# Loading q and k by blocks of 32 tokens with four heads in one DMA, and issuing v half a slot behind its buffer's use

## The chip, the cores and the metric

The kernel runs on one core of a Trainium2 chip. The metric is the device time of one execution in microseconds (us), as the median of several runs. Besides, one execution was taken with the hardware profiler; its trace is what the rows below come from. Times inside the trace count from the start of its span.

## The reference

Attention within chunks of 64 tokens, then two feed-forward layers one after the other. All inputs are float32 but the four weight arrays and alpha, which are float64 on the host.

```python
# q, k, v: (8 batches, 8 heads, 576 tokens, 64)
scores = 1/sqrt(64) * q_c @ k_c^T            # in chunks of 64 tokens
attn = exp(scores - max); attn = attn / (sum(attn) + 1e-9)
out = attn @ v_c
x = out as (8 * 576 = 4608 tokens, 512)      # heads side by side
h = x @ w_in;   x = (h * sigmoid(1.702 h)) @ w_out          # 512 -> 2048 -> 512
h = x @ w_in2;  y = (max(h, 0) + alpha * min(h, 0)) @ w_out2
```

## The kernel before

**Groups, blocks, slots.** Attention works on 36 groups `g` of 128 tokens (`NG`, line 73). A batch has 576 tokens, which is four and a half groups, so the groups 4, 13, 22 and 31 straddle two batches: 64 tokens of one, 64 of the next. The first feed-forward layer works on 9 blocks of 512 tokens (four groups each), and each block has 16 slots `n`, one for each 128 columns of the hidden layer. In a slot TensorE makes 12 matmuls of `emit_h` (line 454) and 12 of `emit_y` (line 477). The second layer (lines 601 to 868) follows when the first is done, and nothing in it is touched here.

**Attention between the slots.** The attention of the groups from 4 on is threaded into the slots by hand: the table `between` (lines 930 to 941) says at which half slot a step of group `g` is emitted, counted from `8 * (g - 4)`. An even half slot lies in the middle of `emit_h` (`middle`, line 951), an odd one behind `emit_y` (line 970). `att_T` (-4) transposes q and k on VectorE (line 325), `att_S` (-1) makes the scores on TensorE (line 341), `att_E` (-1) the exponentials, `att_AT` (2) transposes them, `att_PV` (5) multiplies with v on TensorE (line 410), after which ScalarE copies the result into the layer's input (line 418).

**The loads.** All DMAs are issued by SyncE (SP in the rows), strictly in the order in which the program emits them. `load_qk` (line 285) loads q and k of a group in eight parts, q in parts 0 to 3, k in parts 4 to 7, one part at each half slot from -1 to 6, two groups ahead. In the tile (128 partitions by 512) the partition is 32 columns `y` of a head of even or odd number, so that VectorE's transposes of 32 by 32 give what TensorE needs; line 298 therefore issues one DMA for each head, each `y`, and each batch that the group touches: 4 DMAs of 16 KB in a part, and 8 of 8 KB in a part of a straddling group. The tiles of q and of k have two buffers each, and the first DMA of a tile waits until `att_T` has read the group two before. `load_v` (line 282, issue at line 276) loads v of the next group into the single buffer of v, so it waits for the matmuls of `att_PV`; it is emitted at half slot 7. Groups 4 and 5 are loaded by another list (`LOADS`, line 20), so `load_qk` serves groups 6 to 35, of which 13, 22 and 31 straddle.

**What else is in SP's queue.** The first layer's weights (lines 132 and 137) during the first block; from slot 19 to slot 123, once in 3.25 slots, a step that prepares the second layer's weights: two loads of raw weights (line 202), which ScalarE reads two slots later (line 152), and two stores (line 208) of what ScalarE and GpSimd have made of them; and at each block's end four stores of the layer's result (line 491).

**Order within one half slot.** The list at a half slot holds its steps in the order in which the loop over `g` adds them. With v at half slot 7, the queue of SP has part 7 of k (group g + 2), then v (group g + 1), then part 0 of q (group g + 3).

Of the kernel before, what the change touches and what calls it, by code (L numbers as in the profile page):

```python
# [17 lines left out]
SQ = 32  # L18
# [30 lines left out]
def tile_chunk_attention_two_ffn(  # L49
# [14 lines left out]
    nc = tc.nc  # L64
    B, H, S, D = q.shape
    NT, DM = out.shape
    DFF = w_in1.shape[1]
    P = 128
# [3 lines left out]
    GPB = NB // P  # L72
# [172 lines left out]
    def spans(t0, n):  # L245
        done = 0
        while done < n:
            b, s = divmod(t0 + done, S)
            step = min(n - done, S - s)
            yield done, step, b, s  # L250
            done += step
# [33 lines left out]
    def load_qk(part, g):  # L285

        nm, src = (("q", q), ("k", k))[part // 4]
        if part % 4 == 0:  # L290
            t = qkv_p.tile([P, 512], F32, tag=nm, name=nm, bufs=2)
            qkv[g, nm] = t.rearrange("p (h b e) -> p h b e", h=HP, e=SQ)
        t = qkv[g, nm]
        for h in range(part % 4 * 2, part % 4 * 2 + 2):
            for y in range(D // SQ):
                r = (h % 2) * D + y * SQ
                for off, n, b, s in spans(g * P, P):
                    nc.sync.dma_start(  # L298
                        out=t[r:r + SQ, h // 2, off // SQ:(off + n) // SQ],
                        in_=src[b, h, s:s + n, y * SQ:(y + 1) * SQ].rearrange(  # L300
                            "(b t) e -> t b e", t=SQ
                        ),
                    )

    qkT = {}

# [563 lines left out]
    with tc.manual_schedule():  # L870
# [50 lines left out]
        for i, step in enumerate(steps):  # L921
            n = PREP_FROM + int(i * PREP_EVERY)
# [7 lines left out]
        between = {}  # L930
        for g in range(GPB, NG):
            for at, fn in zip((-4, -1, -1, 2, 5), (att_T, att_S, att_E, att_AT, att_PV)):
                if g > GPB or at > 0:
                    between.setdefault(8 * (g - GPB) + at, []).append((fn, g))
            if g + 1 < NG:
                between.setdefault(8 * (g - GPB) + 7, []).append((load_v, g + 1))
            if g + 2 < NG:
                for part in range(8):
                    between.setdefault(max(0, 8 * (g - GPB) - 1 + part), []).append(
                        (partial(load_qk, part), g + 2)  # L940
                    )
# [83 lines left out]
```

## Time and profile before

| | us |
|---|---|
| median of 3 runs | 1686.51 |
| the three runs | 1685.52 to 1688.97 |
| the profiled execution | 1682.19 |
| its span in the trace | 1680.4 |
| TensorE busy in it | 1610.9 |
| VectorE busy in it | 1243.7 |

The profiled execution is 4.3 us below the median of the runs, and 1.8 us of it lie outside the span. The first layer ends near 930 us of the span, the second takes the rest. In the rows, PE is TensorE, PEld its weight loads, DVE VectorE, ACT ScalarE, POOL GpSimd, SPq the queue of SyncE, by which the DMAs are issued. The duration of a DMA in SPq is the time that SyncE spent on issuing it, not the transfer.

### The profile page before, as it was taken

How to read it: one execution, taken by the hardware profiler on the slowest of the kernel's cores; microseconds unless marked ns; L12 is line 12 of the kernel's file. 1: busy time of each engine (PE TensorE's matmuls, PEld its weight loads, DVE VectorE, ACT ScalarE, POOL GpSimd, SP SyncE). 2: the span in 40 equal slices, each digit the busy share in tenths (PEclk: the TensorE clock that was granted, in tenths of full speed). 3: DMA queues.
4: the chain of work that ended last, by engine and by line, in shares of the span. 5: the costliest groups of instructions: out<-in, count | busy, mean ns of one | idle time of the engine just before them, and what ended most of it. 6: DMA issues, size and time to landing. Idle time of an engine off the chain costs nothing.

```text
span 1680.4 us, 25742 instructions
## 1 busy us (share of the span) xinstructions
PE 1610.9 (96%) x9259; PEld 1342.0 (80%) x9259; DVE 1243.7 (74%) x1858; ACT 782.9 (47%) x1098; POOL 491.4 (29%) x382
## 2 busy tenths in 40 slices
PE   7889998999999999989999999999999999999997
PEld 5667886888877788778888778878887888899897
DVE  7898676677766877767744367987889789788776
ACT  5555344444434444435433364545555555445543
POOL 3665121322222222222202025322523332241220
PEclk8999998999999999999999999999999999999999
DMA  9741333445334444444330376669667866987974
GB/s 235 203 133 18 93 96 101 124 113 133 99 101 114 134 107 114 106 105 129 101 131 14 120 233 192 196 173 303 192 188 180 286 193 201 249 309 231 264 235 134
DMA packets 385582, 268.10 MB, mean 160 GB/s; under 512 B 265648, under 2 KB 323504, under 8 KB 385456
## 3 DMA queue, kind: packets, MB, share of 16 engines
q1 hardware_dynamic: 385456, 266.47, 55.4%
q8 instruction: 73, 1.20, 0.3%
q14 instruction: 53, 0.43, 0.1%
HBM read 218.11 MB, written 48.23 MB: 159 GB/s over the span
## 4 chain that ended last, share of the span: by engine, by line
PE 61%; DVE 16%; SPq 4%; ACT 4%; DMA 3%; issue 3%; POOL 0%; DVEq 0%; ACTq 0%; POOLq 0%
PE psY L477 16%; PE psH L454 15%; PE psHa L653 8%; PE psYa L770 8%; PE psYb L770 6%; PE psHb L653 6%; SPq L298 3%; DVE g L672 3%; DVE o L717 2%; DVE yacc L788 2%; DVE at L393 2%; PE psS L341 2%; DVE g L698 1%; DVE xop L566 1%; DVE g L463 1%
## 5 line engine op out<-in xcount | busy, mean ns | idle before, releaser
L454 PE MATMUL psH<-xs,wi 128*128 128x512 f32 x1728 | 439.3, 405 | 10.2 <-DVE g L463 5.9
L477 PE MATMUL psY<-gs,wo 128*128 128x512 f32 x1728 | 416.4, 391 | 0.1
L454 PEld LDWEIGHTS psH<-xs,wi 128*128 128x128 f32 x1728 | 330.2, 194 | 86.4 <-DVE g L463 9.3
L477 PEld LDWEIGHTS psY<-gs,wo 128*128 128x128 f32 x1728 | 325.4, 189 | 68.7 <-POOL gs L123 0.5
L120 ACT CAST gs<-g 128x512 fp32r<-128x512 f32 x144 | 89.3, 620 | 331.5 <-DVE g L463 331.5
L770 PE MATMUL psYa<-o,w 128*128 128x512 f32 (+1 forms) x960 | 216.2, 371 | 9.9 <-DVE o L717 3.6
L653 PE MATMUL psHa<-xop,wi2t 128*128 128x512 f32 (+1 forms) x960 | 211.8, 369 | 2.6 <-DVE g L698 1.9
L770 PEld LDWEIGHTS psYa<-o,w 128*128 128x128 f32 x960 | 173.7, 188 | 40.7 <-DVE o L717 10.6
L653 PEld LDWEIGHTS psHa<-xop,wi2t 128*128 128x128 f32 x960 | 175.1, 188 | 27.6 <-DVE g L698 2.7
L672 DVE SCALAR_TENSOR_TENSOR g<-neg,minus_alpha,g 128x512 f32<-128x512 f32 (+1 forms) x160 | 179.3, 1161 | 9.9 <-ACT g L669 9.7
L653 PE MATMUL psHb<-xop,wi2t 128*128 128x512 f32 (+1 forms) x720 | 158.8, 369 | 3.2 <-DMA wi2t<-wi 2.3
L770 PE MATMUL psYb<-o,w 128*128 128x512 f32 (+1 forms) x720 | 159.0, 368 | 0.1
L123 DVE TENSOR_TENSOR gs<-g,gs 128x512 fp32r<-128x512 f32 x129 | 91.9, 712 | 88.6 <-ACT gs L120 87.9
L463 DVE TENSOR_TENSOR g<-psH,g 128x512 f32<-128x512 f32 x144 | 98.1, 681 | 79.1 <-ACT g L461 78.2
L653 PEld LDWEIGHTS psHb<-xop,wi2t 128*128 128x128 f32 x720 | 131.3, 188 | 21.5 <-DMA wi2t<-wi 2.9
L722 POOL TENSOR_TENSOR tsum<-g,tsum 128x1024 f32<-128x1024 f32 (+1 forms) x39 | 93.0, 2384 | 187.8 <-DVE o L717 187.8
L722 POOL TENSOR_TENSOR tsum<-g,g 128x1024 f32<-128x1024 f32 (+1 forms) x19 | 42.6, 2243 | 356.0 <-DVE g L672 220.2
L770 PEld LDWEIGHTS psYb<-o,w 128*128 128x128 f32 x720 | 131.3, 188 | 18.2 <-DVE o L717 1.5
L393 DVE STREAM_TRANSPOSE at<-e 32x128 f32<-32x128 f32 x448 | 135.5, 302 | 6.7
L461 ACT ACTIVATE g<-psH 128x512 f32<-128x512 f32 x144 | 86.2, 599 | 74.3 <-PE psH L454 73.6
L668 ACT ACTIVATE neg<-g 128x1024 f32<-128x1024 f32 (+1 forms) x60 | 58.6, 976 | 122.2 <-DVE g L698 122.2
L367 POOL TENSOR_TENSOR e<-e,d 128x512 f32<-128x512 f32 x32 | 33.5, 1046 | 253.9 <-DVE d L366 235.9
(117 smaller groups left out, 1888.3 us busy)
## 6 DMA issues: line engine op xcount, KB each, us to landing
wi2t<-wi SPq DMA_DIRECT2D x280, 256.0 KB, 3.6
w<-wo SPq DMA_DIRECT2D x140, 512.0 KB, 3.8
x<-ysb SPq DMA_DIRECT2D x36, 256.0 KB, 2.6
raw<-in_moe_w_in_dram SPq DMA_DIRECT2D x16, 512.0 KB, 5.4
raw<-in_moe_w_out_dram SPq DMA_DIRECT2D x16, 512.0 KB, 4.3
raw<-in_moe_w_in_dram SPq DMA_DIRECT2D x32, 256.0 KB, 4.0
wi<-stb SPq DMA_DIRECT2D x16, 512.0 KB, 3.0
raw<-in_moe_w_out_dram SPq DMA_DIRECT2D x32, 256.0 KB, 3.6
```

The source lines that it names most:

```text
L120: nc.scalar.copy(hi, src)
L123: eng_lo.tensor_tensor(out=lo, in0=src, in1=hi.bitcast(F32), op=ALU.subtract)
L393: nc.vector.transpose(t[o * SQ:(o + 1) * SQ, :, i * SQ:(i + 1) * SQ], blocks[i * SQ:(i + 1) * SQ, :, o // 2, o % 2, :],)
L454: nc.tensor.matmul(ps, w[:, a, c], xs[:, b, c], start=(i == 0), stop=(i == 3 * KT - 1))
L461: nc.scalar.activation(out=g, in_=ps, func=AF.Sigmoid, scale=1.702)
L463: nc.vector.tensor_tensor(out=g, in0=ps, in1=g, op=ALU.mult)
L477: nc.tensor.matmul(y_t[j][t], w[:, a, t * P:(t + 1) * P], gs[:, b], start=(f == 0 and a + b == 0), stop=(f == NF - 1 and b == 1),)
L653: nc.tensor.matmul(ps, w[:, c, a], x[b][:, c], start=(k == 0 and i in (1, 2, 5)), stop=(k == 5 and i in (2, 3, 4)), skip_group_check=True,)
L668: nc.scalar.activation(out=neg, in_=src, func=AF.Relu, scale=-1.0)
L672: nc.vector.scalar_tensor_tensor(out=g, in0=neg, scalar=minus_alpha[:, f:f + 1], in1=g, op0=ALU.mult, op1=ALU.add)
L722: eng.tensor_tensor(out=wide(homes[out], n), in0=wide(homes[x], n), in1=wide(homes[y], n), op=ALU.subtract,)
L770: nc.tensor.matmul(ps[:, d, :n], w[:, jj, d, a], x[b][:, jj], start=(k == 0 and i in (1, 5, 2)), stop=(k == 5 and i in (3, 2, 4)), skip_gr ...
```

## The change

`load_qk` is rewritten: a part is now a block of 32 tokens instead of a pair of heads. It makes one DMA for each parity of the head number and each half `y` of the head's columns, and a DMA takes the four heads of that parity at once: 4 DMAs of 16 KB in every part of every group, straddling or not, since 32 divides 576 and no block of 32 tokens crosses a batch. The pieces of 128 bytes are as before; in the tile they now lie 512 bytes apart, in the input one head pair apart. Then `load_v` is emitted at half slot 6 instead of 7: in SP's queue v (group g + 1) goes ahead of part 7 of k (group g + 2).

```diff
-        for h in range(part % 4 * 2, part % 4 * 2 + 2):
+        off = part % 4 * SQ
+        b, s = divmod(g * P + off, S)
+        for par in range(2):
             for y in range(D // SQ):
-                r = (h % 2) * D + y * SQ
-                for off, n, b, s in spans(g * P, P):
-                    nc.sync.dma_start(
-                        out=t[r:r + SQ, h // 2, off // SQ:(off + n) // SQ],
-                        in_=src[b, h, s:s + n, y * SQ:(y + 1) * SQ].rearrange(
-                            "(b t) e -> t b e", t=SQ
-                        ),
-                    )
+                r = par * D + y * SQ
+                nc.sync.dma_start(
+                    out=t[r:r + SQ, :, part % 4],
+                    in_=src[b, par::2, s:s + SQ, y * SQ:(y + 1) * SQ].rearrange("h t e -> t h e"),
+                )
...
             if g + 1 < NG:
-                between.setdefault(8 * (g - GPB) + 7, []).append((load_v, g + 1))
+                between.setdefault(8 * (g - GPB) + 6, []).append((load_v, g + 1))
```

## Rows read from the trace of the kernel before

**Rows 1.** The page: busy us (share), instructions.
```profile
PE 1610.9 (96%) x9259; PEld 1342.0 (80%) x9259; DVE 1243.7 (74%) x1858; ACT 782.9 (47%) x1098; POOL 491.4 (29%) x382
```

**Rows 2.** Timeline, PE: att_PV of groups 11, 15, 19, 23, 27, 31, 35.
```profile
246.91 0.69 PE L410 MATMUL psX<-at,v 64*64 64x64 f32 x32
...
353.78 0.69 PE L410 MATMUL psX<-at,v 64*64 64x64 f32 x32
...
450.29 0.69 PE L410 MATMUL psX<-at,v 64*64 64x64 f32 x32
...
555.07 0.69 PE L410 MATMUL psX<-at,v 64*64 64x64 f32 x32
...
651.54 0.69 PE L410 MATMUL psX<-at,v 64*64 64x64 f32 x32
...
756.07 0.69 PE L410 MATMUL psX<-at,v 64*64 64x64 f32 x32
...
852.74 0.69 PE L410 MATMUL psX<-at,v 64*64 64x64 f32 x32
```

**Rows 3.** Waits of PE, 168 to 900 us: total, times, longest.
```profile
PE psS L341 <- ACT x L418: 9.4, 4, 4.4
PE psX L410 <- DMA v<-in_v_dram: 5.8, 3, 2.3
```

**Rows 4.** Busy us by stretch, PE to POOL, then PEclk, DMA share, GB/s.
```profile
235.00:269.00 34.00, 34.00 (x203) 27.16 (x202) 23.22 (x49) 14.27 (x25) 8.41 (x13) 1.00 0.28 67
269.00:291.00 22.00, 15.72 (x106) 12.30 (x105) 12.79 (x30) 5.67 (x10) 1.23 (x1) 0.77 0.53 148
315.00:340.00 25.00, 25.00 (x166) 20.32 (x165) 16.57 (x36) 11.72 (x19) 6.44 (x8) 1.00 0.47 120
```

**Rows 5.** Timeline of SP, straddling group 13: start, us, engine, line.
```profile
257.43 11.82 SPq L298 DMA_DIRECT2D k<-in_k_dram  x24
269.35 0.39 SPq L276 DMA_DIRECT2D v<-in_v_dram  x1
...
280.45 1.54 SPq L202 DMA_DIRECT2D raw<-in_moe_w_in_dram  x2
```

**Rows 6.** Timeline of SP in a group that doesn't straddle.
```profile
409.91 2.02 SPq L298 DMA_DIRECT2D k<-in_k_dram  x4
412.03 0.38 SPq L276 DMA_DIRECT2D v<-in_v_dram  x1
```

**Rows 7.** Timeline of PE there: att_PV of groups 17 and 18.
```profile
402.44 0.69 PE L410 MATMUL psX<-at,v 64*64 64x64 f32 x32
...
426.37 0.69 PE L410 MATMUL psX<-at,v 64*64 64x64 f32 x32
```

**Rows 8.** Timeline of ACT, straddling group 22; in brackets the idle time.
```profile
506.14 0.67 ACT L152 ACTIVATE u<-raw 128x512 f32<-128x512 f32 x1 [7.69 <-DMA q<-in_q_dram]
```

**Rows 9.** Timeline of DVE: the transpose of group 19's q.
```profile
426.18 0.70 DVE L325 STREAM_TRANSPOSE qT<-q 128x512 f32<-128x512 f32 x1
```

**Rows 10.** Issues on SP by line: duration ns min/median/max, first and last start.
```profile
L298 SPq DMA_DIRECT2D q<-in_q_dram x528: 311/430/1713, 37.2 to 803.0; - x176
...
L805 SPq DMA_DIRECT2D out_dram<-x_t x64: 348/502/1422, 1128.3 to 1576.4; - x64
...
L202 SPq DMA_DIRECT2D raw<-in_moe_w_in_dram x32: 545/608/1755, 186.2 to 501.9; - x32
```

**Rows 11.** Waits of SP's queue, the whole span: total us, times, longest.
```profile
SPq L276 <- PE psX L410: 24.9, 2, 17.0
```

**Rows 12.** Waits of SP's queue, 168 to 850 us.
```profile
SPq L208 <- POOL sums L238: 25.8, 13, 4.2
SPq L208 <- POOL sta L226: 24.7, 5, 10.3
...
SPq L208 <- POOL stb L226: 19.4, 8, 7.7
```

**Rows 13.** DMA issues: count, KB each, median us to landing.
```profile
q<-in_q_dram SPq DMA_DIRECT2D x96, 8.0 KB, 1.8
```

## The prediction

> **What bounds the kernel now.** I read the busy times first: TensorE is busy 96% of the span, and no other engine is above 74% [rows 1]. So only what makes TensorE wait, or slows it, is worth anything, and the change touches the first layer alone. Next I took the timeline of TensorE and marked the same step, `att_PV`, once for every four groups, which is one block. The marks [rows 2] give the block times 106.87, 96.51, 104.78, 96.47, 104.53 and 96.67 us. The reader is to see an alternation: three blocks of about 96.5 us, and three that are longer by 10.3, 8.2 and 8.0 us. The long ones are those in which q and k of the straddling groups 13, 22 and 31 are loaded, two groups ahead of their use.
>
> Then I asked what TensorE waits for there. From 168 to 900 us there are two waits that count: v's DMA, three times, 5.8 us, and ScalarE's copy of the attention's result, 9.4 us [rows 3]. Three waits on v for three straddling groups. The stretch of the first of them has TensorE busy 15.72 of 22 us and at a mean granted clock of 0.77, while a regular stretch has 25.00 of 25 at 1.00 [rows 4]. So a part of the excess is work done at the lower of the two clock levels (1.2 instead of 2.4 GHz) behind the idle time; it goes when the idle time goes, as the stretches at 1.00 on either side show.
>
> SP's timeline gives the reason. It issues 24 DMAs of k without a break for 11.82 us, only then v at 269.35, and the raw weights of the preparation at 280.45 [rows 5]. That is 0.49 us for each DMA, whatever its size. The second wait hangs on the same queue: in group 22 ScalarE idles 7.69 us ahead of its operation on the raw weights [rows 8], because those stand behind q's DMAs in the queue, and ScalarE's copy for TensorE stands behind that operation.
>
> The count closes. A straddling group has 64 DMAs of q and k, 64 * 0.49 = 31.5 us of SP. Beside them stand v (0.39 us) and, 4 / 3.25 = 1.2 times in a group of four slots, a preparation step of two loads and two stores, at most 4 * 0.61 = 2.4 us if all cost what the dearer of them do [rows 10], so 3.0 us. That makes 34.9 us, where a group lasts 96.5 / 4 = 24.1. SP is 10.8 us over; the observed 8.0 to 10.3 is this, less some lead. A regular group needs 32 * 0.49 + 3.4 = 19.1 us and fits.
>
> **The change, part by part.**
>
> *Fewer DMAs.* Removed: in each of three straddling groups 64 issues become 32; the 96 DMAs of 8 KB for q [rows 13] become 48 of 16 KB, and so do k's, 96 issues fewer in all. Per group that is 32 * 0.49 = 15.7 us of SP time, which is more than the overload of 10.8 us, so the group becomes a regular one. Nothing then leaves v late or the raw weights late: v's regular lead is 10 us (below), and what is late next is nothing on SP, since regular blocks run TensorE with no wait on it. What it brings is the excess of the three long blocks over 96.5: 10.3 + 8.2 + 8.0 = 26.5 us. The first layer is a chain on TensorE and the second starts from its end, so all of this reaches the end.
>
> *The other form of the DMA, in all 30 groups.* Count, bytes and pieces (128 bytes) are the same in the 27 regular groups. Changed is that the pieces in the tile lie apart and that they come from four heads. The trace has no such load, so I bound SP's price for it. Low end: the same as now, median 430 ns [rows 10]; the 8 KB form of the straddling groups, with other sizes, took the same pace [rows 5]. Middle: the 128-byte output stores, with pieces apart on one side, 502 ns. High end: the raw weights' loads, whose tile side is also in pieces for one of each two, 608 ns. What there is to spend is SP's idle time in the prepared stretch: it waits for GpSimd's results 25.8 + 24.7 + 19.4 = 69.9 us [rows 12], over some 26 groups 2.7 us a group, or 0.08 us for each of 32 DMAs. The low end costs nothing; the middle, 0.07 us more, still fits (2.3 of 2.7 us); the high end, 0.18 us more, is 5.7 us a group, 3.0 over. I take the low end, because 430 ns holds for 8 KB and 16 KB alike and for all positions in the tile. A gain below nothing isn't excluded (the fastest took 311 ns), but SP has idle time in regular groups already, so it would bring no time. Landing: SP hides it as long as it comes before the data's use, and q and k are read some 12 us later (next part).
>
> *v half a slot earlier.* In a regular group v is issued at 412.03 right behind the four DMAs of part 7 (409.91 on) [rows 6]. Its buffer became free at 402.44 + 0.69 = 403.13, and it is read at 426.37 [rows 7]. So v now comes 2.1 us earlier, still 6.8 us after its buffer is free: SP doesn't wait for it. TensorE has no wait on v outside the straddling groups, so the 2.1 us are worth nothing. What v is moved past is part 7, four DMAs of k; they go 0.4 us later, and their first reader is the transpose at 426.18 [rows 9], 12 us on: hidden. Where SP does wait for v's buffer, twice in the whole span, 24.9 us [rows 11], it is ahead of its work; there four DMAs that stood before the wait come after it, 2 us that SP makes up from that same idle time. Price between 0 and 2 us once or twice, taken as 0, since part 7's readers lie a group away.
>
> **Sum.** -26.5 + 0 + 0 = -26.5 us. Against the profiled execution: 1682.2 - 26.5 = 1655.7 (span 1680.4 to 1653.9). The profiled execution is 4.3 us under the median of the runs, and the predicted median is 1686.5 - 26.5 = 1660.0 us.
>
> **Rivals.**
>
> *The issue of the new form is dear, and SP becomes the bound everywhere* (slower than before). The place is the 26 groups with preparation, the price what exceeds 2.7 us of idle time. At 608 ns it is 3.0 us * 26 = 78 us, less the 26.5: +52, 1738 us. It breaks even where a group is 1.0 us over, 3.7 / 32 = 0.12 us more than now: the mechanism decides from 0.55 us an issue on. For it: the raw loads show such prices, and SP has little to spare. Against it: rows of the same size as ours are all near 430. A form of it: the part's writes are taken to overlap those of the part before in the same partitions, and each DMA waits for the landing of the fourth before; with 1.8 us to landing [rows 13] and four issues of 0.49 between, that wait is near nothing. Together 0.07.
>
> *The transfers bind, not their issue* (no change). Then the same pieces take the same time and the excess stays: 1686.5. Against it: in the straddling stretch the DMA engines are busy 0.28 of the time, in a regular one 0.47 [rows 4]; they are starved there, not full. The Trainium skill, "DMA: Bandwidth & Descriptors", section "Issuing engines are not separate DMA queues", says that the time on the sequencer to initiate a DMA is usually small relative to the DMA itself; by that rule halving the issues would bring nothing. Here it doesn't hold for these small DMAs, by the shares just named. Chance 0.04.
>
> *Only a part is won.* SP has little slack, and the new form may cost 0.1 us more: then the straddling groups still become regular, but each prepared group loses some tenths of a us, 3.2 - 2.7 = 0.5 * 26 = 13, net -13.5: 1673 us. Chance 0.12.
>
> *More is won.* The 0.4 us by which the regular blocks differ, or the start, where v or weights come earlier: at most some 5 us, 1655. Little speaks for it: at the start SP itself waits for `att_PV`, 24.9 us in two waits [rows 11], so it is ahead of the work there and not behind it. Chance 0.03.
>
> **How the numbers follow.** The forecast has 0.74. Its own spread is small: the three runs lie within 3.5 us, and the choice of the regular block moves the sum by 0.6. The low end, 1653, takes in the case of more; the high end, 1673, takes in the partial case. What is left out is about 0.13. A difference under 0.2% (3.4 us) can hardly be told from no change: faster 0.88 (forecast, partial, more: 0.89, less a little for partial cases that end within 3.4 us), same 0.05, slower 0.07.
>
> **What would show it.** Right: the blocks from group 11 to 35 all last near 96.5 us; no wait of `att_PV` on v; the granted clock stays at 1.00 from 170 to 900 us; SP issues 960 DMAs at line 298 or its successor, of 16 KB, near 0.43 us. v is issued 2 us earlier after `att_PV`, and nothing gains from it. Wrong: an issue above 0.5 us and fewer waits of SP for GpSimd, then waits of ScalarE on raw weights in regular groups; or long blocks that stay at the same three places, then it was not the count of issues.

## The result, and the profile after

| | before | after |
|---|---|---|
| median of the runs, us | 1686.01 (4 runs, 1682.88 to 1688.97) | 1660.47 (4 runs, 1656.31 to 1662.30) |
| ratio, 95% interval | | 0.9838, 0.9818 to 0.9858 |
| span of the profiled execution, us | 1680.4 | 1658.2 |

The change makes the kernel 25.5 us faster by the medians, and 27.3 us by the ratio of the table; the quotient of the two medians, 0.985, lies inside its interval. 1660.0 was forecast. In the profile after, all line numbers from `load_qk` on are lower by one, and the loads of q and k are at line 299.

TensorE's busy time and the rest, from the page of after; it answers to [rows 1]:

```profile
PE 1601.7 (97%) x9259; PEld 1336.9 (81%) x9259; DVE 1239.9 (75%) x1858; ACT 782.4 (47%) x1098; POOL 494.0 (30%) x382
```

The timeline of TensorE in the kernel after, `att_PV` of groups 11, 15, 19, 23, 27, 31 and 35, as in [rows 2]:

```profile
246.87 0.69 PE L409 MATMUL psX<-at,v 64*64 64x64 f32 x32
...
342.89 0.69 PE L409 MATMUL psX<-at,v 64*64 64x64 f32 x32
...
439.38 0.69 PE L409 MATMUL psX<-at,v 64*64 64x64 f32 x32
...
535.85 0.69 PE L409 MATMUL psX<-at,v 64*64 64x64 f32 x32
...
632.31 0.69 PE L409 MATMUL psX<-at,v 64*64 64x64 f32 x32
...
728.78 0.69 PE L409 MATMUL psX<-at,v 64*64 64x64 f32 x32
...
825.48 0.69 PE L409 MATMUL psX<-at,v 64*64 64x64 f32 x32
```

The blocks now last 96.02, 96.49, 96.47, 96.46, 96.47 and 96.70 us. The reader is to see that group 11 stands at 246.9 in both kernels, and that the three long blocks, and only they, have lost 10.85, 8.31 and 8.06 us: 27.2 in all. The first layer ends at 951.6 us of the span in the kernel before (not near 930, as was said ahead of the prediction) and at 924.3 in the kernel after.

The waits of TensorE from 168 to 900 us in the kernel after (total, times, longest), against [rows 3]:

```profile
PE psX L409 <- DVE at L392: 2.4, 7, 0.5
PE psS L340 <- ACT x L417: 0.2, 1, 0.2
```

v's DMA is gone from the list, and the wait for ScalarE's copy has shrunk from 9.4 to 0.2 us. The same stretches as in [rows 4], in the kernel after:

```profile
235.00:269.00 34.00, 34.00 (x206) 27.80 (x205) 26.46 (x60) 14.60 (x25) 9.66 (x13) 1.00 0.45 118
269.00:291.00 22.00, 21.77 (x152) 17.57 (x151) 15.54 (x35) 9.99 (x16) 5.47 (x7) 1.00 0.48 118
```

In the second one TensorE is busy 21.77 of 22 us instead of 15.72, at a granted clock of 1.00 instead of 0.77. The DMA engines' share in the first one rises from 0.28 to 0.45, near the 0.47 of the regular stretch. Over the six blocks from group 11 to group 35, before and then after:

```profile
246.91:852.74 605.83, 588.13 (x3841) 475.26 (x3840) 428.39 (x909) 260.59 (x424) 148.48 (x199) 0.98 0.43 112
246.87:825.48 578.61, 576.51 (x3842) 467.56 (x3841) 428.36 (x909) 260.30 (x424) 148.36 (x199) 1.00 0.45 116
```

The same matmuls take 27.2 us less. TensorE's idle time falls from 17.7 to 2.1 us, which is 15.6 of them; the other 11.6 are busy time, 588.1 against 576.5 us, with the granted clock at 0.98 against 1.00. So a good part of the excess was work at the lower clock behind the waits, and it went with them.

SP's timeline there, in the kernel after, beside [rows 5]:

```profile
253.07 0.39 SPq L276 DMA_DIRECT2D v<-in_v_dram  x1
253.50 2.00 SPq L299 DMA_DIRECT2D k<-in_k_dram  x4
...
269.70 1.54 SPq L202 DMA_DIRECT2D raw<-in_moe_w_in_dram  x2
```

v is issued at 253.07 instead of 269.35, ahead of the last four DMAs of k, and the raw weights at 269.70 instead of 280.45. The issue of q's DMAs, by line, and their landing, in the kernel after [rows 10, 13]:

```profile
L299 SPq DMA_DIRECT2D q<-in_q_dram x480: 311/430/1838, 36.4 to 776.6; - x160
...
q<-in_q_dram SPq DMA_DIRECT2D x480, 16.0 KB, 2.0
```

The new form has the same median price as the old one, 430 ns, and so have k's 480 DMAs. That makes the 960 DMAs of 16 KB that were forecast.

### The profile page after: what moved, and what is told of

Read it like the earlier page. It is cut to its first block, busy times and chain, and to the rows that moved or that the text cites. A ratio compares the mean times of both kernels' runs of the same rounds, so it can differ in the third digit from the quotient of the medians.

```text
span 1658.2 us, 25643 instructions
## 1 busy us (share of the span) xinstructions
PE 1601.7 (97%) x9259; PEld 1336.9 (81%) x9259; DVE 1239.9 (75%) x1858; ACT 782.4 (47%) x1098; POOL 494.0 (30%) x382
## 4 chain that ended last, share of the span: by engine, by line
PE 68%; DVE 15%; ACT 3%; issue 3%; SPq 2%; DMA 2%; POOL 0%; DVEq 0%; ACTq 0%; POOLq 0%
PE psY L476 19%; PE psH L453 18%; PE psHa L652 8%; PE psYa L769 8%; PE psYb L769 6%; PE psHb L652 5%; DVE g L671 3%; DVE yacc L787 2%; DVE o L716 2%; PE psS L340 2%; DVE at L392 2%; DVE g L697 1%; DVE xop L565 1%; SPq L804 1%; PE psX L409 1%
## 5 line engine op out<-in xcount | busy, mean ns | idle before, releaser
L453 PE MATMUL psH<-xs,wi 128*128 128x512 f32 x1728 | 430.0, 399 | 11.3 <-DVE g L462 8.5
L453 PEld LDWEIGHTS psH<-xs,wi 128*128 128x128 f32 x1728 | 324.1, 191 | 84.3 <-DVE g L462 11.1
```

Source lines behind the costliest of these rows:

```text
L453: nc.tensor.matmul(ps, w[:, a, c], xs[:, b, c], start=(i == 0), stop=(i == 3 * KT - 1))
```

## The experiments

Theory A is the prediction's: in the three straddling groups SP has more to issue than a group's time holds, and what comes late in its queue stops TensorE. The rivals: it is v's place in the queue, or the new order of the pieces, or the DMAs themselves wherever they are issued. Each run's ratio stands against runs of the kernel before on the same chip.

**e1: the new loads alone.**

```diff
-                between.setdefault(8 * (g - GPB) + 6, []).append((load_v, g + 1))
+                between.setdefault(8 * (g - GPB) + 7, []).append((load_v, g + 1))
```

> The new loads of q and k, with v left at half slot 7. Theory A (the count of issues on SP in the three straddling groups is all): as the changed kernel, 1660 us, ratio to before 0.984 +- 0.002; v is issued some 2 us later behind att_PV than in the changed kernel and still lands near 8 to 10 us before its use. Rival (v's earlier issue carries part of the gain): above 1664 us, with waits of att_PV on v's DMA left in the trace.

Measured: 1660.15 us, ratio 0.9833 (0.9811 to 0.9855). The whole gain is in the loads of q and k, and no wait on v's DMA is left in its trace.

**e2: v's place alone.** The loads of the kernel before, with

```diff
-                between.setdefault(8 * (g - GPB) + 7, []).append((load_v, g + 1))
+                between.setdefault(8 * (g - GPB) + 6, []).append((load_v, g + 1))
```

> The old loads of q and k, with v at half slot 6. In a straddling group v then goes ahead of 8 DMAs of k, 8 * 0.49 = 3.9 us earlier, which is more than the 1.3 to 2.3 us that att_PV waited for it. Theory A: these waits go, but the raw weights of the preparation come as late as before, ScalarE idles on them as before, and TensorE's waits move to att_S behind ScalarE's copy; 1680 to 1687 us, that is 0 to 6 us won. Rival (the wait on v was the main part of the excess, with the lower clock that follows it): 15 us or more won, below 1672 us.

Measured: 1688.03 us, ratio 0.9998 (0.9982 to 1.0015): nothing. That is 1 us above the range that was expected, and at its end of no gain, since the kernel before took 1687.96 us on that chip. TensorE's waits, 168 to 900 us, in this run:

```profile
PE psS L341 <- ACT x L418: 17.8, 5, 7.0
PE psX L410 <- DVE at L393: 3.6, 7, 1.6
```

and SP's timeline in its first straddling group:

```profile
259.15 8.05 SPq L298 DMA_DIRECT2D k<-in_k_dram  x16
267.30 0.39 SPq L276 DMA_DIRECT2D v<-in_v_dram  x1
267.73 3.87 SPq L298 DMA_DIRECT2D k<-in_k_dram  x8
...
281.80 1.54 SPq L202 DMA_DIRECT2D raw<-in_moe_w_in_dram  x2
```

The wait on v is gone, as it should be, and its time has moved on: the wait for ScalarE's copy grew from 9.4 [rows 3] to 17.8 us. The raw weights come as late as before (281.80 against 280.45 [rows 5]), ScalarE idles on them, and TensorE is held one step later instead of one step earlier. Here two waits that hang on one late queue don't add up; to remove the first gives its time to the second.

**e3: the new loads in the straddling groups alone**, the old ones in the 27 others, v at half slot 7.

```diff
+        if len(list(spans(g * P, P))) == 2:
+            ...the four DMAs of the changed kernel
+            return
         for h in range(part % 4 * 2, part % 4 * 2 + 2):
```

> The new loads in groups 13, 22 and 31 alone, the old ones in the 27 others, v at half slot 7. Theory A: only these groups were overloaded, so as the changed kernel, 1660 us, ratio 0.984; blocks of 96.5 us. Rival (the new form helps or costs something in every group): differs from the run with the new loads everywhere by more than 3 us.

Measured: 1660.63 us, ratio 0.9834 (0.9806 to 0.9863). In the 27 other groups the new form neither helps nor costs anything that these runs can tell.

**e4: the new form with the old count in the straddling groups.**

```diff
+                step = 2 if len(list(spans(g * P, P))) == 2 else HP
+                for h in range(0, HP, step):
...
-                    out=t[r:r + SQ, :, part % 4],
+                        out=t[r:r + SQ, h:h + step, part % 4],
```

> As the changed kernel, but in groups 13, 22 and 31 a DMA takes two heads instead of four, so that there are again 64 issues of 8 KB; the pieces, their places and the order of the tokens are those of the changed kernel. Theory A (the count of issues): the three long blocks come back, 104 to 107 us each, the gain goes, 1680 to 1688 us; v still comes 3.9 us earlier there, so up to 6 us may stay. Rival (the new order of the pieces, or the transfers themselves, brought the gain): 1660 us as the changed kernel.

Measured: 1689.45 us, ratio 1.0015 (1.0001 to 1.0029). TensorE's timeline, `att_PV` of groups 11, 15, 19 and 23 (line numbers are higher by one than before):

```profile
246.67 0.69 PE L411 MATMUL psX<-at,v 64*64 64x64 f32 x32
...
352.25 0.69 PE L411 MATMUL psX<-at,v 64*64 64x64 f32 x32
...
448.71 0.69 PE L411 MATMUL psX<-at,v 64*64 64x64 f32 x32
...
555.31 0.69 PE L411 MATMUL psX<-at,v 64*64 64x64 f32 x32
```

Blocks of 105.58, 96.46 and 106.60 us: the long ones are back, with the pieces in the new order. So the order of the pieces is not it. What came back is the count, and with it DMAs of half the size; e8 parts these two. The median lies 1.5 us above the upper end of what was expected. In the profiled execution the first layer is not longer than that of the kernel before by more than 1 us (it ends at 952.4 against 951.6 us), and the second one is (last section).

**e5, e6, e7: 36, 40 and 48 issues in every group.** The prediction's dear-issue rival rested on one number, SP's idle time of 2.7 us a group. These runs add issues of the same bytes until it is used up.

```diff
+                step = 2 if r == 0 and part % 2 else HP      # e5: 36
+                step = 2 if r == 0 else HP                   # e6: 40
+                step = 2 if par == 0 else HP                 # e7: 48
+                for h in range(0, HP, step):
```

> As the changed kernel, but in each odd part one DMA of four heads is cut into two of two heads: 36 issues in every group instead of 32, same bytes, pieces and places. The step under test is the idle time of SP that the prediction put at 2.7 us a group. Theory A: 4 * 0.49 = 2.0 us more fit into it, so 1660 us, no change against the changed kernel. Rival (SP has no room, each added issue counts): 2.0 us * 26 groups = 51 us, 1711 us.

> One DMA cut in two in every part: 40 issues in every group. 8 * 0.49 = 3.9 us more than now, against idle time of SP of 2.7 us (by the waits before the change) to 3.2 us (the waits for GpSimd after it, 82.5 us over 26 groups). Theory A: over by 0.7 to 1.2 us in 26 groups, 18 to 31 us, that is 1678 to 1691 us, with ScalarE waiting for raw weights in regular groups. Rival (SP's lead of whole slots takes it up, or the waits for GpSimd aren't the whole of its room): within 3 us of the changed kernel.

> Two DMAs cut in two in every part: 48 issues in every group, 7.8 us more. Theory A: over by 4.6 to 5.1 us in 26 groups, 120 to 133 us, 1780 to 1793 us. Rival (the overload shows only in part, since groups without preparation and block ends give some back): 1720 to 1760 us; or none: 1660 us.

| issues in a group | median, us | ratio to before, 95% interval |
|---|---|---|
| 32 (the kernel after) | 1660.47 | 0.9838, 0.9818 to 0.9858 |
| 36 | 1661.48 | 0.9837, 0.9822 to 0.9853 |
| 40 | 1687.21 | 0.9994, 0.9976 to 1.0011 |
| 48 | 1780.47 | 1.0543, 1.0523 to 1.0562 |

Four more cost nothing that can be measured, eight more cost 27 us, the whole gain, and sixteen 120 us. From 40 to 48 it is 93 us in 26 groups, 3.6 us for 8 issues or 0.45 us for each, against the 0.49 us that one takes: past the edge an issue costs nearly its full time. At 40 the cost is 26.7 / 26 = 1.0 us a group of the 3.9 us added, so SP had some 2.9 us of idle time that it could use; 2.7 had been read from its waits. These waits of SP's queue, 168 to 850 us, in the kernel after and then at 40 issues:

```profile
SPq L490 <- ACT ysb L489: 50.5, 7, 24.8
SPq L208 <- POOL sums L238: 43.9, 18, 5.5
SPq L208 <- POOL stb L226: 21.0, 10, 7.6
SPq L208 <- POOL sta L226: 17.6, 5, 10.6
```

```profile
SPq L208 <- POOL sta L226: 10.2, 1, 10.2
SPq L492 <- ACT ysb L491: 9.5, 1, 9.5
SPq L208 <- POOL stb L226: 7.6, 2, 6.1
...
SPq L208 <- POOL sums L238: 1.6, 5, 0.5
```

The waits for GpSimd (POOL), which the prediction and the expectations counted, fall from 82.5 to 19.4 us. Beside them stands a wait that they left out, for ScalarE ahead of the stores at a block's end; it is the longest of all and falls from 50.5 to 9.5 us. So SP's idle time is more than its waits for GpSimd, and how much of it more issues can use is told by these runs and not by the list. In place of the waits ScalarE waits for raw weights in the regular groups, at 40 issues (total, times, longest):

```profile
ACT u L152 <- DMA raw<-in_moe_w_out_dram: 27.9, 12, 4.6
ACT u L152 <- DMA raw<-in_moe_w_in_dram: 21.8, 13, 4.0
```

against 1.3 and 2.7 us in the kernel after.

**e8: the same 64 DMAs, half of them issued by GpSimd.** The kernel before, with

```diff
-                    nc.sync.dma_start(
+                    (nc.gpsimd if nm == "k" and n < P else nc.sync).dma_start(
```

> The kernel before, with one thing changed: in groups 13, 22 and 31 the 32 DMAs of k are issued by GpSimd instead of SP. The count of DMAs, their bytes, pieces and places are those of the kernel before. Theory A (SP's issue time binds): SP has 32 issues left there, 15.7 + 3.4 = 19.1 us of 24.1, and the gain comes as with the changed kernel, 1660 us, or up to 1670 us if GpSimd's own work falls behind. Rival (what binds is the DMAs themselves, wherever they are issued): 1686 us.

Measured: 1667.05 us, ratio 0.9867 (0.9846 to 0.9889). The issues, by line:

```profile
L298 POOL DMA_DIRECT2D k<-in_k_dram x96: 533/536/702, 241.3 to 702.7; - x96
```

All 64 DMAs still run, with 8 KB each, and 22.5 us come, where the new form with 36 issues won 28.1 us on the same chip. So it is SP's time for the issue that binds, not the DMAs. Some 6 us are missing, and the trace has them in the same three blocks, which last 101.1, 98.4 and 97.5 us. GpSimd has taken k's issues, but q's 32 stand as before on SP in one half of the group, 15.7 us of issues in 12 us. In the first straddling group the raw weights are issued behind 24 of them:

```profile
247.03 1.23 SPq L202 DMA_DIRECT2D raw<-in_moe_w_in_dram  x2
```

In the kernel before this was at 247.13, in the kernel after at 241.70. ScalarE waits for them here, and does not in the kernel after (second line):

```profile
252.95 0.67 ACT L152 ACTIVATE u<-raw 128x512 f32<-128x512 f32 x1 [4.76 <-DMA raw<-in_moe_w_in_dram]
248.04 0.67 ACT L152 ACTIVATE u<-raw 128x512 f32<-128x512 f32 x1
```

From 168 to 850 us ScalarE waits 15.2 us for raw weights in this run, against 4.0 in the kernel after. This account of the missing part is read from the trace; no run tried it by itself.

**e9: SP stays overloaded, its readers get more lead.** The kernel of e2, with the raw weights loaded one slot earlier.

```diff
-                ("prep", 1, prep_load), ("abs", 3, prep_abs), ("prep", 3, prep_decode),
+                ("prep", 0, prep_load), ("abs", 3, prep_abs), ("prep", 3, prep_decode),
```

> As the run with v alone moved (old loads, 64 issues in a straddling group, v at half slot 6), and the raw weights' loads of every preparation step emitted one slot earlier. SP stays overloaded for the time of a straddling group, but both of its impatient readers now have more lead: in such a group a slot holds 16 DMAs of q and k, 16 * 0.49 = 7.8 us, and ScalarE waited 6.2 to 8.3 us. Theory A (the overload costs only by what comes late; it would be taken up by lead): the long blocks shrink to 97 to 100 us, 1664 to 1675 us. Rival (an overloaded SP must stretch the group anyway, by some other reader that then comes late): blocks stay at 104 us or more, 1682 us or more.

Measured: 1671.07 us, ratio 0.9895 (0.9873 to 0.9917), with all 64 issues on SP. TensorE's waits, 168 to 900 us:

```profile
PE psX L410 <- DMA v<-in_v_dram: 4.3, 2, 2.7
PE psX L410 <- DVE at L393: 2.8, 7, 1.0
```

The time is as expected; of the blocks one is not. The first long block is gone (95.7 us), the second is left with 102.0 us, above the 97 to 100 expected, and the third with 98.2, where v comes late once more behind the raw weights that now stand ahead of it. The regular block from group 31 to 35 is longer too, 98.6 us, which was not followed up. So two thirds of the gain come with SP as loaded as before: the overload of the three groups can for the most part be carried by lead, and costs where a reader's lead is shorter. Fewer issues are still the better way by some 10 us, and no run was clearly faster than the changed kernel.

## Why the prediction was right

- **The bound.** Three long blocks, all their excess due to SP: right. They lost 27.2 us by the marks where 26.5 were summed, and the medians differ by 25.5. That the median came out within 0.5 us of the forecast is luck: the runs of the kernel after lie 6 us apart.
- **Fewer issues.** Right, and shown from three sides: the form alone without the count brings nothing (e4), the count in the three groups alone brings all (e3), and taking half of the issues off SP brings most of it with all DMAs in place (e8). The lower clock went with the idle time: the stretch rose from 0.77 to 1.00, and over the six blocks 11.6 of the 27.2 us were busy time.
- **The count of SP's time.** Right in its direction, looser than it looks. By the prediction's sum a regular group leaves SP 24.1 - 19.1 = 5.0 us idle; by its reading of the waits it is 2.7 us, and that reading leaves out the wait ahead of the block-end stores (in the kernel before `SPq L491 <- ACT ysb L490: 22.3, 5, 11.1`). The runs with 36 and 40 issues put what can be used at some 2.9 us, and so a straddling group at 15.7 - 2.9 = 12.8 us too much instead of 10.8. So "the count closes" is less exact than 10.8 against 8.0 to 10.3 looks: by this more of the overload was carried by lead than the sum has. The forecast doesn't rest on it, since its 26.5 us come from the marks.
- **The new form's price.** The low end was taken, 430 ns, and is what was measured. The high end, 608 ns, would have cost 5.7 us a group; e6 shows that 3.9 us a group already takes the gain away, so the rival's threshold, 3.7 us more for the break-even, was of the right size: 40 issues came out at 0.9994.
- **v's place.** Worth nothing, as said: e1 leaves it out and has the same time. In regular groups it came 1.7 us earlier, not 2.1: v at 399.38, behind `att_PV` of group 17 at 391.54. The lead of 10 us that the prediction gives v isn't worked out there; from issue to use the rows give 426.37 - 412.03 = 14.3 us [rows 6, 7], before the landing is taken off.
- **What was read less sharply.** The prediction listed the wait on v and the wait for ScalarE's copy side by side, 5.8 and 9.4 us. It had not said that they replace one another. e2 shows it: without the first the second is 17.8 us.
- **The rule of the Trainium skill.** The Trainium skill, "DMA: Bandwidth & Descriptors", section "Issuing engines are not separate DMA queues", says that issuing from several engines saves only the sequencer's time to initiate a DMA, which is usually small relative to the DMA itself. The prediction said that this doesn't hold here. For one DMA it does: a median of 0.43 us to issue, and 1.8 us to the landing of 8 KB [rows 10, 13]. What did not hold is the step from there to "fewer issues bring nothing". The issues follow one another every 0.49 us, while a transfer is still under way when the next is issued, so that 64 issues were the bound with the DMA engines busy 0.28 of the time; and to save only the sequencer's time, in e8, was worth 22.5 us.
- **The profiled execution** was put at a span of 1653.9 us and came out at 1658.2. The first layer kept to the sum; the second took longer, as the last section tells.

## What to carry to other kernels

Count the issues of the queue that loads for a stretch, times the time of one issue, and set it against the length of the stretch: how near a queue is to its limit shows in the idle time that it has left, and not yet in waits of the engine that it feeds; past the edge each issue here cost nearly its full time. Look at the odd cases, here the groups that straddle a boundary and need twice the DMAs; cutting blocks so that they never straddle removes them without moving a byte less. Where two waits hang on the same late queue, removing one of them can win nothing, as in e2, and that does not clear the queue.

## What was not expected of the hardware

The second layer, untouched, lasted 728.8 us in the profiled execution of before and 733.9 in that of after (spans less the ends of the first layer, 951.6 and 924.3 us); over the profiled runs of all kernels here it ranges from 727.6 to 735.9. Set side by side, the same matmuls run 27.3 us earlier in after than in before at the layer's start, 25.4 us earlier behind one place and 22.1 behind a second; elsewhere the distance hardly moves. The first place, TensorE's timeline, before and then after:

```profile
1456.69 1.31 PE L653 MATMUL psHb<-xop,wi2t 128*128 128x384 f32 x6 [1.11 <-DMA wi2t<-wi]
1459.90 2.32 PE L770 MATMUL psYa<-o,w 128*128 128x384 f32 x12 [1.89 <-DMA w<-wo]
```

```profile
1429.81 1.32 PE L652 MATMUL psHb<-xop,wi2t 128*128 128x384 f32 x6 [1.18 <-DMA wi2t<-wi]
1433.20 3.64 PE L769 MATMUL psYa<-o,w 128*128 128x384 f32 x12 [2.07 <-ACT neg L667]
```

TensorE idles 1.11 and 1.89 us ahead of these matmuls before, and 1.18 and 2.07 after; then twelve matmuls take 2.32 us in the one and 3.64 in the other. The granted clock over them is 1.00 before; after it is 0.62, a mean of the levels of 1.2 and 2.4 GHz:

```profile
1433.00:1437.00 4.00, 3.80 (x14) 3.83 (x15) 0.13 (x1) 1.03 (x2) 0.00 (x0) 0.62 1.03 405
```

The second place, before and then after:

```profile
1582.94 2.34 PE L770 MATMUL psYa<-o,w 128*128 128x384 f32 x12 [1.00 <-DMA w<-wo]
1559.54 3.61 PE L769 MATMUL psYa<-o,w 128*128 128x384 f32 x12 [2.63 <-DMA w<-wo]
```

Here too the clock falls to a mean of 0.62 in after alone, behind idle time that is 1.6 us longer. The lower clock thus makes 1.3 us at each place, 2.6 of the 5.1 us; most of the rest is idle time at the second place. At the first, idle times that differ by a quarter of a microsecond went with the full clock in one trace and with the lower one in the other. Two traces don't show that this quarter tipped it, and what does stays open. Places like these can be a part of why the second layer's time moves by several us between executions; no run was made to settle that.
